# Another order of products at the seams of a two-level Winograd kernel, two attention steps placed earlier, and weight quarters stored in rows of 1 KB

## The chip, the cores and the metric

The kernel runs on one core of a Trainium2 chip. TensorE (PE in the profile) multiplies matrices and writes its results to banks of PSUM; VectorE (DVE), ScalarE (ACT) and GpSimd (POOL) work on them element by element; SyncE (SP) issues the DMAs, one after another in a fixed order. The time of a kernel is the device time of one execution in microseconds (us); times that are compared are medians of several runs. Everything is computed in float32, or in float32r with operands split into parts.

## The reference

A retention layer (linear attention with a decaying state) is followed by a feed-forward layer with ELU:

```python
# q, k, v: (4 batches, 8 heads, 768 positions, 64)
for t in range(S):
    state = gamma * state + k[t] v[t]^T        # per head, 64 x 64
    y[t] = q[t] state / sqrt(64)
x = y as (3072 tokens, 512)                    # the heads side by side
h = x @ w_in                                   # (3072, 2048)
g = where(h > 0, h, exp(min(h, 0)) - 1)
out = g @ w_out                                # (3072, 512)
```

## The kernel before

**Work.** The 3072 tokens are six blocks of 512, each of four chunks of 128. Retention is computed by chunks: scores (k^T q inside stretches of 64 tokens, masked; `scores`, L336), the products k^T v that carry the state (`states`, L385), and the outputs from both (`outputs`, L397). Each is a train of 64x64 matmuls: `scores(tb, pp)` and `states(tb, pp)` treat pair `pp` of the chunks of block `tb`. Their sums and masks are VectorE's (L342, L383), the decay of v is POOL's (`scale_v`, L305).

The two products of the feed-forward layer use Winograd's form of Strassen's scheme: seven products of quarter blocks instead of eight, with sums of blocks before and after. The numbers 1 to 7 in the code name these seven products. Block 0 takes `plain_first` and `second_of_first`. Block 1 takes one level in the first layer (`first(n)`, four entries n = 0 to 3, L772, steps in `strassen`, L734) and two levels in the second (`second_twice`, L953). Blocks 2 and 3, then 4 and 5, are taken together in two **rounds** (`for nb in range(NB)`).

**A round.** In a round's first layer the outer products 2, 1, 3 and 7 are done by a second level, in eight **units** (`ORDER1`: four products, two halves each), each a generator `big_twice` (L1255). Outer products 4 and 6 are done in float32r: `passes` (L1323) multiplies weights and inputs that were split into a high and a low part. Per 128 rows of outputs there is a slice A (first passes of 6, `six`), B (first passes of 4, `four`) and C (the third pass of both). Outer product 5 (`big_rest`, L1309) is plain float32. The **entry** is the place where the units end and the passes begin. After the first passes of a slice VectorE scales the bank and adds another term (`six_sum`, `four_sum`, L917), and only then may the third pass add to that bank. `begin` and `end` are the two halves of an ELU: ScalarE's two operations (L1342, L1343), then VectorE's (L1344). `seeds` are POOL's sums (L1833 to L1837) at the entry. The round's second layer is `second_big` (L1361).

**Inside a unit.** Products 1, 6, 5 and 3 write to bank `pa` (two of these, taken in turn), 2 to `pb`, 7 and 4 to `pd`. ScalarE copies what is needed later (`lift`, L1279), VectorE adds (`plus`, L1283). The unit stops at each `yield`; the loop over `ORDER1` runs the new unit (`cur`) to its next stop, and in between the rest of the one before (`tail`). By that, before the change TensorE's order at a seam is 1 of the new unit, 4 of the old, 2, 6, 7 of the new, 3 of the old, 5 of the new.

**Queues.** The order on every engine is written by hand, by the order of the calls. Weights come in slices of 128x512 or 128x256 from DRAM through a ring of eight buffers (`wq`; eleven in the first layers). `want_first` (L1160) and `want_second` list the slices in the order of use; `done` gives a buffer back when TensorE has read it, and `fetch` (L850) then issues the next slice on the list. SyncE handles its DMAs strictly in order, so a fetch that waits for TensorE holds up what is queued behind it: stores (`send_small`, L679), outputs, and the loads of chunks (`load`, L125). Eight semaphores serve the DMAs in turn, so that each DMA also waits for the landing of the one eight before.

**Parts.** `parts_of_layer` (L919) splits a quarter of a weight block into three planes: ScalarE (L923), VectorE (L917), POOL or VectorE (L925), and two stores. `next_part` (L1701) sends the planes made last and makes the next; it uses two buffers `wp`, so it waits for an earlier store to land. Six of the eight parts are made while `first(1)` to `first(3)` run, in the loop at L1706.

**Raw quarters.** `send_quarters` (L897) stores the blocks of `w_in` for the second round's units, of which product 1 and 2 use halves of one slice (`scratch3[.., 0]`), and product 4 half of another. The first round reads these blocks straight from `w_all`.

Of the kernel before, what the change touches and what calls it, by code (L numbers as in the profile page):

```python
# [28 lines left out]
def kernel(  # L29
# [645 lines left out]
    to_send = []  # L675
# [221 lines left out]
    def send_quarters(j):  # L897

        for at in range(2):
            for k, n, half in ((1, 0, 0), (2, 0, 1), (4, 2, 1)):  # L900
                r, c = {1: (0, 0), 2: (0, 1), 4: (1, 1)}[k]
                to_send.append((
                    scratch3[AMONG[j], at, n][:, 256 * half : 256 * half + 256].rearrange("p (f d) -> p f d", f=2),
                    W_IN[j][:, 2 * r + at, :, c, :],
                ))
# [254 lines left out]
    def want_first(n):  # L1160
# [20 lines left out]
        piece(*before, 3)  # L1181
        for m in range(2 * NQ):
            part("C", m)
            part("B", m)
            if m + 1 < 2 * NQ:
                part("A", m + 1)
            if n and m % 2:
                want((tb, "r", 5, m // 2), scratch4[m // 2])
# [66 lines left out]
    def big_twice(n, j, at):  # L1255
# [3 lines left out]
        def product(k, ps, begin):  # L1259
            which, half = AT[k]  # L1260
            name = (n + 2, "t", j, at, which)
            if n == 0 and k in (1, 2, 4):
                r, c = {1: (0, 0), 2: (0, 1), 4: (1, 1)}[k]
                w = W_IN[j][:, 2 * r + at, :, c, :]
            else:
                w = where[name][:, 256 * half : 256 * half + 256].rearrange("p (f d) -> p f d", f=2)
# [26 lines left out]
        u2 = lift(pa)  # L1293
        pd = bank("d")
# [411 lines left out]
    for n in range(NQ):  # L1706
# [8 lines left out]
        for at in range(2):  # L1715
            next(cur)
        next(tail, None)
# [11 lines left out]
        for at, s in enumerate(cur):  # L1729
            next(sides[n], None)  # L1730
            next(sides[n], None)
            if n and at:
                next_part(n < 3)
# [47 lines left out]
    for s in sec:  # L1781
# [11 lines left out]
        if at in LOADS:  # L1793
            load(3 * CPB + LOADS[at])
            scale_v(3 * CPB + LOADS[at])
        if s == ORDER2[-1]:
            break
    scores(3, 0)
# [8 lines left out]
    for nb in range(NB):  # L1807
# [82 lines left out]
        for at, (j, sub) in enumerate(ORDER1):  # L1890
# [13 lines left out]
            next(cur)  # L1904
            side(at, 1)
            if nb == 0:
                if at == 0:
                    states(3, 0)
                elif at == 1:
                    retention_step(3, 3)  # L1910
            run(tail)
            if at == 7:
                seeds(0, 1, first=True)
            next(cur)
            tail = cur
            if nb == 0:
                if at == 0:
                    scores(3, 1)
# [17 lines left out]
        end("C11", 5)  # L1936
        for n in range(2 * NQ):
# [10 lines left out]
            four(n)  # L1948
# [3 lines left out]
            if n < LAST:  # L1952
                six(n + 1)
            if n:
# [7 lines left out]
            elif n == 1:  # L1962
                end("C11", 6)
            else:
                end("C22", n - 2)
            if n:
                end("C21", n - 1)
# [111 lines left out]
```

## Time and profile before

| | us |
|---|---|
| median of 3 runs | 613.16 |
| the runs | 612.36, 615.98, 613.16 |
| the profiled execution | 612.33 |
| its span | 610.6 |

The stretches of the profiled execution, by the windows of the trace (us from the span's start; shares of the window):

| stretch | what runs there | VectorE busy | DMA share |
|---|---|---|---|
| 133.5 to 190 | `first`, block 1's first layer | 0.88 | 0.87 |
| 190 to 237 | `second_twice` | 0.86 | 0.91 |
| 237 to 259 | first two units, with block 4's retention | 0.75 | 0.64 |
| 259 to 295 | units, round one | 0.90 | 0.94 |
| 295 to 333 | passes, round one | 0.93 | 0.85 |
| 333 to 432 | second layer, round one | 0.82 | 0.59 |
| 432 to 484 | units, round two | 0.73 | 0.52 |
| 484 to 523 | passes, round two | 0.92 | 0.70 |
| 523 to 610 | second layer, round two | 0.77 | 0.54 |

TensorE counts as busy over nearly the whole span, and its granted clock is 1.0 throughout. A float32 matmul of the program is two records in the trace (x8 is a product of four), a float32r one is one record. In the order of time a line shows the start and the length in us, the engine, the line of code, the operation, what it writes and reads, the shapes, how many were merged, and in brackets the idle time before it with what ended it. In the list of waits a line shows who waited for whom, with the total in us, the number of times and the longest. Because matmuls are pipelined, a matmul's own length (379 ns for 128x256) is longer than the distance to the next one (216 ns).

### The profile page before, as it was taken

The page shows a single profiled execution, that of the slowest core. Times are in us where ns is not written, and L with a number is a line of the kernel's source. Part 1 is how long each engine was busy: PE and PEld are TensorE (multiplying, and loading weights), DVE is VectorE, ACT ScalarE, POOL GpSimd, SP SyncE. Part 2 cuts the span into 40 slices and gives each one's busy share as a digit, 9 for nine tenths or more (in the row PEclk, how much of TensorE's full clock was granted, in tenths as well). Part 3 has the DMA queues.
Part 4 walks back from the last instruction along what each step waited for, and adds up shares of the span by engine and source line. Part 5 has one row for each costly group of instructions (what it writes and reads, how often), then busy time and mean ns, then how long its engine had stood idle before and what let it go on. Part 6 is the DMA issues. An engine that isn't in the chain of part 4 may idle for free.

```text
span 610.6 us, 13767 instructions
## 1 busy us (share of the span) xinstructions
PE 602.7 (99%) x5510; PEld 492.5 (81%) x5510; DVE 506.5 (83%) x778; ACT 262.3 (43%) x448; POOL 97.0 (16%) x75
## 2 busy tenths in 40 slices
PE   8999999999999999999999999999999999999997
PEld 6765568888889998888766888888888866788886
DVE  5769889989799886889998787898658999778785
ACT  6899744205553112147689310100236778611110
POOL 2011000000220001000697000110000398000000
PEclk9999999999999999999999999999999999999999
DMA  8698569789977999599986455874554676656553
GB/s 318 272 389 308 172 215 270 234 244 259 353 236 242 296 394 325 182 299 258 307 286 222 125 136 156 271 272 115 191 166 154 172 206 191 166 152 188 152 151 116
DMA packets 87856, 139.85 MB, mean 229 GB/s; under 512 B 7024, under 2 KB 48752, under 8 KB 83056
## 3 DMA queue, kind: packets, MB, share of 16 engines
q1 hardware_dynamic: 87792, 138.96, 71.3%
q8 instruction: 44, 0.72, 0.5%
q14 instruction: 20, 0.16, 0.1%
HBM read 105.12 MB, written 33.82 MB: 228 GB/s over the span
## 4 chain that ended last, share of the span: by engine, by line
PE 92%; DMA 3%; DVE 2%; POOL 1%; issue 0%; ACT 0%; ACTq 0%; DVEq 0%
PE pa L1376 16%; PE pa L1268 8%; PE pd L1376 8%; PE pa L977 4%; PE pb L1376 4%; PE pd L1268 4%; PE pa L557 3%; PE x L647 3%; PE pa L784 3%; PE x L1330 3%; PE pa L647 2%; PE pa L1317 2%; PE pb L1268 2%; PE sc L331 2%; PE pd L977 2%; PE kv L371 2%
## 5 line engine op out<-in xcount | busy, mean ns | idle before, releaser
L1384 ACT COPY ms<-pa 128x256 f32<-128x256 f32 x41 | 15.2, 372 | 107.5 <-PE pa L1376 103.0
L1376 PE MATMUL pa<-gC,wq 128*128 128x256 f32 x240 | 56.8, 382 | 0.0
L1376 PEld LDWEIGHTS pa<-gC,wq 128*128 128x128 f32 x240 | 45.1, 190 | 7.2 <-issue 1.0
L305 POOL TENSOR_TENSOR chunk<-chunk,vf 128x512 f32<-128x512 f32 x15 | 19.1, 1278 | 164.9 <-DMA chunk<-in_qkv_dram 120.2
L1343 ACT ACTIVATE r<-r 128x512 f32<-128x512 f32 x64 | 40.4, 631 | 2.0
L1279 ACT COPY m<-pa 128x512 f32<-128x512 f32 x32 | 18.7, 584 | 38.5 <-PE pa L1268 35.1
L1388 DVE TENSOR_TENSOR res<-pd,ms 128x256 f32<-128x256 f32 x26 | 11.0, 422 | 28.2 <-PE pd L1376 17.4
L1376 PE MATMUL pd<-w_all,wq 128*128 128x256 f32 x120 | 28.3, 379 | 0.0
L1344 DVE SCALAR_TENSOR_TENSOR gC<-r,gC 128x512 f32<-128x512 f32 x24 | 27.6, 1158 | 0.0
L925 POOL TENSOR_TENSOR wp<-wp 128x512 fp32r<-128x512 f32 x6 | 8.4, 1404 | 116.3 <-DMA scratch_dram<-wi 102.8
L1376 PEld LDWEIGHTS pd<-w_all,wq 128*128 128x128 f32 x120 | 22.8, 190 | 3.1
L1833 POOL TENSOR_TENSOR chunk<-chunk,w_all 128x512 f32<-128x512 f32 x4 | 5.1, 1298 | 127.1 <-DVE gC L1348 127.1
L183 ACT ACTIVATE w_all<-wraw 128x1024 uint32<-128x1024 uint32 (+1 forms) x19 | 19.1, 1007 | 14.0 <-PE x L647 9.8
L1358 DVE TENSOR_TENSOR gC<-w_all,gC 128x1024 f32<-128x1024 f32 x20 | 24.2, 1260 | 0.0
L1376 PE MATMUL pa<-ts,wq 128*128 128x256 f32 x96 | 22.9, 381 | 0.0
L1376 PE MATMUL pa<-w_all,wq 128*128 128x256 f32 x96 | 22.9, 381 | 0.0
L185 ACT ACTIVATE w_all<-wraw 128x1024 fp8e4<-128x1024 f32 (+1 forms) x19 | 22.6, 1190 | 0.6
L1376 PE MATMUL pd<-ts,wq 128*128 128x256 f32 x96 | 22.7, 379 | 0.0
L557 PE MATMUL pa<-xb,w_all 128*128 128x512 f32 x48 | 21.5, 597 | 0.0
L1410 ACT COPY res<-pa 128x256 f32<-128x256 f32 x13 | 4.8, 372 | 38.1 <-PE pa L1376 38.1
L213 DVE CUSTOM_DVE_ANT_0 w_all<-wraw,w_all 128x2048 uint16<-128x2048 uint16 (+1 forms) x19 | 20.1, 1057 | 0.8
L514 ACT ACTIVATE r<-r 128x512 f32<-128x512 f32 x32 | 20.2, 630 | 1.0
(361 smaller groups left out, 1606.7 us busy)
## 6 DMA issues: line engine op xcount, KB each, us to landing
wq<-scratch_dram SPq DMA_DIRECT2D x231, 256.0 KB, 3.5
chunk<-in_qkv_dram SPq DMA_DIRECT2D x22, 1024.0 KB, 7.3
wraw<-in_w_dram SPq DMA_DIRECT2D x15, 1024.0 KB, 6.1
scratch_dram<-wp SPq DMA_DIRECT2D x8, 512.0 KB, 4.0
out_dram<-res SPq DMA_DIRECT2D x7, 512.0 KB, 3.4
scratch_dram<-gT SPq DMA_DIRECT2D x12, 256.0 KB, 4.3
wq<-scratch_dram SPq DMA_DIRECT2D x24, 128.0 KB, 3.2
scratch_dram<-w_all SPq DMA_DIRECT2D x24, 128.0 KB, 3.0
```

Source lines behind the costliest of these rows:

```text
L183: nc.scalar.activation(flat, lo, AF.Copy, scale=2.0**-29)
L185: nc.scalar.activation(top, hi.bitcast(FP32), AF.Copy, scale=2.0**-120, saturate=False)
L213: vec.tensor_tensor(out=flat, in0=c, in1=flat, op=ALU.add)
L514: nc.scalar.activation(e, e, AF.Exp, scale=-1.0)
L557: nc.tensor.matmul(hp, lhsT=w[n][:, fi, j // 2, j % 2, :], rhs=xb[:, j, :], start=(j == 0), stop=(j == 3))
L647: nc.tensor.matmul(X[j][:, d, :], lhsT=w[j][:, d * P : d * P + P], rhs=x[j], start=(n == 0 and d == 0), stop=at_end, skip_group_check=True,)
L977: nc.tensor.matmul(ps, lhsT=w[:, f, :], rhs=ts[j][k][:, f, :], start=(begin and f == 0), stop=(f == 3), skip_group_check=True,)
L1268: nc.tensor.matmul(ps[:, f, :], lhsT=w[:, f, :], rhs=big_xs[j][k], start=(begin and f == 0), stop=True, skip_group_check=True,)
L1343: nc.scalar.activation(r, r, AF.Exp, scale=-1.0)
L1344: return lambda: nc.vector.scalar_tensor_tensor(g, r, -1.0, h, ALU.add, ALU.max)
L1358: nc.vector.tensor_tensor(out=quarter(to, r, t), in0=quarter(x, r, t), in1=quarter(y, r, t), op=op)
L1376: nc.tensor.matmul(ps, lhsT=w[:, f, :], rhs=ts[j][k][:, f // 2, f % 2, :], start=(begin and f == 0), stop=(f == 3), skip_group_check=True,)
```

## The change

1. `send_quarters`: the two blocks that share a slice go out in one store whose rows are 1 KB; the slice then holds them interleaved, and `product` reads its half by another index. Per unit pair there are four stores instead of six.
2. `big_twice` gets one more stop, after product 6. With the changed loop the order at a seam becomes 1 of the new unit, 4 of the old, 2, 6 of the new, 3 of the old, 7, 5 of the new (at the last unit, 3 stays behind 7).
3. `first`: the third entry makes one part less, and the fourth makes one more, between its product 1 and the third entry's product 3.
4. Block 4 (`tb` 3): `scores(3, 0)` moves from the end of `second_twice` to the end of its step 4, `states(3, 0)` from the first unit to the end of step 5, and `scores(3, 1)` from behind product 5 of the first unit to ahead of it.
5. The entry: `four(0)` comes ahead of the first third pass and `four(1)` ahead of the first `four` third pass; the list of slices follows (A0, B0, C0, A1, B1, C1, A2, C2, B2 and on instead of A0, C0, B0, A1, C1, B1). Of two ELU ends in one step, the one whose bank is needed first comes first.

```diff
--- before.py
+++ after.py
@@ -897,12 +897,13 @@
     def send_quarters(j):
 
         for at in range(2):
-            for k, n, half in ((1, 0, 0), (2, 0, 1), (4, 2, 1)):
-                r, c = {1: (0, 0), 2: (0, 1), 4: (1, 1)}[k]
-                to_send.append((
-                    scratch3[AMONG[j], at, n][:, 256 * half : 256 * half + 256].rearrange("p (f d) -> p f d", f=2),
-                    W_IN[j][:, 2 * r + at, :, c, :],
-                ))
+            for k, n in ((slice(2), 0), (1, 2)):
+                w = W_IN[j][:, at if n == 0 else 2 + at, :, k]
+                to = scratch3[AMONG[j], at, n]
+                if n:
+                    to_send.append((to[:, 256:512].rearrange("p (f d) -> p f d", f=2), w))
+                else:
+                    to_send.append((to.rearrange("p (f c) -> p f c", f=2), w.rearrange("p f k d -> p f (k d)")))
 
     LAYER = {4: w_b_[:, :, :, 1], 5: w_b_[:, :, :, 0], 6: w_y_}
 
@@ -1179,9 +1180,15 @@
         part = lambda x, m: want((tb, x, m), scratch5[m, "ABC".index(x)])
         part("A", 0)
         piece(*before, 3)
+        part("B", 0)
         for m in range(2 * NQ):
             part("C", m)
-            part("B", m)
+            if m == 0:
+                part("A", 1)
+                part("B", 1)
+                continue
+            if m > 1:
+                part("B", m)
             if m + 1 < 2 * NQ:
                 part("A", m + 1)
             if n and m % 2:
@@ -1263,7 +1270,11 @@
                 r, c = {1: (0, 0), 2: (0, 1), 4: (1, 1)}[k]
                 w = W_IN[j][:, 2 * r + at, :, c, :]
             else:
-                w = where[name][:, 256 * half : 256 * half + 256].rearrange("p (f d) -> p f d", f=2)
+                w = where[name]
+                if which:
+                    w = w[:, 256 * half : 256 * half + 256].rearrange("p (f d) -> p f d", f=2)
+                else:
+                    w = w.rearrange("p (f k d) -> p f k d", f=2, k=2)[:, :, half]
             for f in range(2):
                 nc.tensor.matmul(
                     ps[:, f, :], lhsT=w[:, f, :], rhs=big_xs[j][k], start=(begin and f == 0), stop=True,
@@ -1291,6 +1302,7 @@
         plus(0, 0, pb, m1)
         product(6, pa, False)
         u2 = lift(pa)
+        yield
         pd = bank("d")
         product(7, pd, True)
         m7 = lift(pd)
@@ -1714,6 +1726,8 @@
         cur = first(n)
         for at in range(2):
             next(cur)
+        if n == 3:
+            next_part()
         next(tail, None)
         next(cur)
 
@@ -1729,7 +1743,7 @@
         for at, s in enumerate(cur):
             next(sides[n], None)
             next(sides[n], None)
-            if n and at:
+            if n and at >= (1, 2, 1)[n - 1]:
                 next_part(n < 3)
             if at == 1 and n == 0:
                 some(smalls[2], 2)
@@ -1793,9 +1807,12 @@
         if at in LOADS:
             load(3 * CPB + LOADS[at])
             scale_v(3 * CPB + LOADS[at])
+        if at == (4, "end"):
+            scores(3, 0)
+        elif at == (5, "end"):
+            states(3, 0)
         if s == ORDER2[-1]:
             break
-    scores(3, 0)
     for _ in sec:
         pass
     mid.close()
@@ -1902,20 +1919,22 @@
             if at == 1 and nb == 0:
                 retention_step(3, 2)
             next(cur)
+            if at < 7:
+                run(tail)
+            next(cur)
             side(at, 1)
             if nb == 0:
                 if at == 0:
-                    states(3, 0)
+                    scores(3, 1)
                 elif at == 1:
                     retention_step(3, 3)
-            run(tail)
             if at == 7:
+                run(tail)
                 seeds(0, 1, first=True)
             next(cur)
             tail = cur
             if nb == 0:
                 if at == 0:
-                    scores(3, 1)
                     states(3, 1)
                 elif at == 1:
                     retention_step(3, 4)
@@ -1934,6 +1953,7 @@
         seeds(2, 3, 4, 5, 6, 7)
         six_sum(0)
         end("C11", 5)
+        four(0)
         for n in range(2 * NQ):
 
             passes(nb, n, 6, True, q6[n])
@@ -1945,12 +1965,15 @@
                 begin("C22", n - 2)
             elif n == 0:
                 begin("C11", 6)
-            four(n)
+            if n > 1:
+                four(n)
             if n > 2:
                 end("C12", n - 3)
             four_sum(n)
             if n < LAST:
                 six(n + 1)
+            if n == 0:
+                four(1)
             if n:
                 begin("C21", n - 1)
                 big_rest(nb, n - 1, q6[n - 1])
@@ -1960,11 +1983,11 @@
                 end("C11", 2)
                 end("C11", 3)
             elif n == 1:
+                end("C21", 0)
                 end("C11", 6)
             else:
-                end("C22", n - 2)
-            if n:
-                end("C21", n - 1)
+                for x, m in (("C21", n - 1), ("C22", n - 2))[:: 1 if n % 2 else -1]:
+                    end(x, m)
             if n == 2:
                 end("C11", 7)
             if n > 1:
```

## The prediction, made before the changed kernel was run

> **What bounds the kernel.** I read the page first, then who waited for whom on TensorE, then TensorE's instructions in order of time around each place that the change touches.
>
> ```profile
> span 610.6 us, 13767 instructions
> PE 602.7 (99%) x5510; PEld 492.5 (81%) x5510; DVE 506.5 (83%) x778; ACT 262.3 (43%) x448; POOL 97.0 (16%) x75
> ...
> q8 instruction: 44, 0.72, 0.5%
> ```
>
> TensorE is busy for 602.7 of 610.6 us. The change neither adds nor removes a matmul, so it can only win back what TensorE loses between matmuls. The busy figure hides part of that, because a matmul's modelled end overlaps the next. I therefore go by the distance from start to start: a 128x256 float32 product runs in steps of 216 ns (eight in 1.73 us), a float32r pass in steps of 232. Whatever exceeds this is loss, plus some 100 ns on the step after a wait.
>
> The waits on TensorE between 160 and 310 us, and the same places in the order of time:
>
> ```profile
> PE y L427 <- issue: 0.6, 1, 0.6
> PE sc L331 <- issue: 0.5, 1, 0.5
> ...
> PE pa L784 <- ACT m L726: 0.2, 1, 0.2
> ```
>
> ```profile
> 242.68 1.08 PE L331 MATMUL sc<-chunk 64*64 64x64 f32 x57
> 244.22 0.34 PE L331 MATMUL sc<-chunk 64*64 64x64 f32 x7 [0.46 <-issue]
> ...
> 247.47 0.93 PE L427 MATMUL y<-chunk 64*64 64x64 f32 x48
> 248.96 0.46 PE L427 MATMUL y<-chunk 64*64 64x64 f32 x16 [0.56 <-issue]
> ```
>
> **1. Fourth entry of `first`: a part moved from the third to the fourth.** ScalarE between 166 and 170 us:
>
> ```profile
> 167.13 0.63 ACT L923 ACTIVATE wp<-w_all 128x512 fp32r<-128x512 f32 x1 [2.80 <-DMA scratch_dram<-wp]
> 167.67 0.57 ACT L726 COPY m<-pa 128x512 f32<-128x512 f32 x1
> 169.09 0.63 ACT L923 ACTIVATE wp<-w_all 128x512 fp32r<-128x512 f32 x1 [0.86 <-DMA scratch_dram<-wp]
> 169.63 0.58 ACT L743 COPY pb<-pa 128x512 f32<-128x512 f32 x1
> ```
>
> The part (L923) waits for a store of its buffer to land, and the two copies that TensorE needs stand behind it. TensorE's steps lose 346+104 ns at 168.29 and 145+104 at 170.26: 0.70 us. In the new order both copies of the third entry stand ahead of the part. Product 5 ends at 166.2, so its copy runs from 166.4 to 167.0 and product 3 starts at 167.95 without waiting. L743 follows the part that ends at 167.76, once product 1 has ended (about 168.1 to 168.7); product 2 wants it at 169.7. **-0.70** (bounds -0.70 and 0). The last part still starts at about 173.1 to 173.6, so SyncE's first fetches behind its store don't get later; their first slice landed 2.4 us before its use.
>
> **2. Scores and k^T v of block four.** Both waits above lie in trains of 64x64 matmuls (64 records in about 1 us), and their steps are 674 and 774 ns too long: 1.45 us. They stand 258 instruction words apart in the program (four words to a float32 matmul, one to a wait), and the 44 packets of the instruction queue are 16 KB each, 256 words. Two start at 241.82 and 246.65 and take 0.92 and 0.96; TensorE goes on 1.5 and 1.4 us after each ends. So a block that is run through in less than the lag to its fetch's start (2.7 and 3.2 us here), plus 0.95, plus 1.4 waits. In words the waiting boundaries follow blocks of 4.3 and 3.7 us. In the new order scores(3,0) and states(3,0) stand a step earlier each among products of the third block, in blocks of 7.7, 7.7 and 10 us, and the first waiting boundary is gone; the second follows a block of 4.7 to 4.8 us. At the lags seen it needs 5.0 to 5.5. I take 0.4 us of stall (bounds 0 and 3.3, by the longest lag seen, 4.8).
>
> Rule and row differ here. The Trainium skill (Runtime: NRT & Kernel Launch, "Instruction fetch mechanics") has the same 16 KiB blocks of 256 instructions, but calls the cost of crossing one mostly hidden; no row shows another cause for these two waits, so I follow the row, and the rule's result is rival A.
>
> Costs. One visit more: three trains become four, and a visit costs 94 ns on the step before, 105 on the step after, and 0.08 us (64 records alone take 1.09, within a longer train 1.01): +0.28. The second scores need the last chunk. Its request (SyncE, 233.67) stands behind a fetch that waits for TensorE at 232.21. Both moved trains now run before that, 1.29 us each, so the request goes out at about 236.1, while scores(3,1), now ahead of product 5, reaches that chunk at 242.3. A chunk lands 5.0 us after its request (310.71) to 8.2 (233.67): 241.1 to 244.3. I take 0.1 us, nearest to the rows with little queued ahead (5.0 to 6.5), as the later fetches leave the queues emptier; bounds 0 and 2.0. VectorE gets 1.3 us of sums with each moved train, and TensorE is later by as much: the slack of 0.28 us at pd (read until 225.51, rewritten at 225.78) stays. Sum: -1.45+0.28+0.10+0.40 = **-0.67** (bounds -1.2 and +1.6).
>
> **3. Seams between units.** A unit's product 1 needs the bank of the unit two before it, whose product 3 came just one product earlier (0.86 us), and ScalarE's copy takes 0.1+0.585 plus its signal. The first step of each such product 1 is 295 to 298 ns instead of 216 (276.03, 282.16, 288.28; 447 to 478 five times), and 267.16, 269.89 and 459.18 lose 138, 134 and 124. With product 3 ahead of product 7 it has two products of cover, and pd's sum three instead of two. Product 5 keeps two behind 6. Round one -0.51, round two -0.53: **-1.04** (bounds -1.04 and 0: the copy of 7 now has two products instead of three, enough for 0.7 us). The waits at 260.85, 262.71 and 439.91 are of another order and stay. VectorE's and POOL's orders don't change here.
>
> **4. The rounds' entry.** TensorE and then VectorE:
>
> ```profile
> 296.20 1.02 PE L1268 MATMUL pa<-w_all,wq 128*128 128x256 f32 x4
> 297.23 0.73 PE L1330 MATMUL pa<-xr,wq 128*128 128x512 f32 x2
> ...
> 299.76 0.73 PE L1330 MATMUL pd<-xl,wq 128*128 128x512 f32 x2
> 300.69 0.73 PE L1330 MATMUL pb<-xr,wq 128*128 128x512 f32 x2 [0.20 <-DVE pb L917]
> ```
>
> ```profile
> 296.47 0.70 DVE L917 SCALAR_TENSOR_TENSOR pa<-pa,chunk 128x512 f32<-128x512 f32 x1 [0.31 <-PE pa L1330]
> ...
> 300.54 2.88 DVE L1344 SCALAR_TENSOR_TENSOR gC<-r,gC 128x512 f32<-128x512 f32 x2
> 303.35 0.69 DVE L917 SCALAR_TENSOR_TENSOR x<-x,m 128x512 f32<-128x512 f32 x1
> ```
>
> Each third pass waits for a sum on VectorE that reads the bank just filled; from 294.4 to 300.7 TensorE takes 6.29 us for 5.44 of steps. The new order puts four(0) and four(1), 0.93 us each, into these gaps. C0 then starts at 297.99 (its sum ends at 297.17), the copy at 299.25, its sum at 300.0; six(1) and four(1) fill up to 300.32; C1 ends at 301.25 as before, with four(1) already done: 0.93 won. But VectorE's two sums of 300.54 stay, so the next sum ends at 304.04, and TensorE would want it at 303.9: some 0.2 given back, and a 0.1 restart. C21's sum now stands ahead of C11's, so four(2) starts at 305.35 rather than 305.92. Round two, whose slices land early: -0.60. In round one B1's slice takes the place of one that landed at 300.06, behind a chunk, and is wanted at 299.39, which leaves -0.35. Two small waits before four(4) go, 72 and 55 ns. **-1.08** (bounds -2.0 and 0).
>
> POOL is the reason for the 2.88 us: L1344 takes 0.68 where POOL is between operations and 1.18 to 1.78 while one runs, ending 0.55 us after it. The Trainium skill (SBUF — State Buffer, "Who interferes with whom") says that a VectorE instruction with two SBUF inputs waits out a running GpSimd one that reads SBUF; the trace agrees. By that rule any sum moved ahead in this queue may cost a POOL operation (1.28 us by its rows): rival C.
>
> **5. Rows of 1 KB.** Twenty-four stores become sixteen, and eight issues of about 0.45 us leave SyncE. Bytes and matmuls are the same. A 128 KB store in 512-byte rows lands 0.37 us after the one before, in 1 KB rows (xb) 0.33. Nothing on TensorE waits for these stores: 0 (bounds -0.2 and 0); one fetch also goes out ahead of two wp stores, which costs nothing, as its slice was already seconds early.
>
> **Sum.** -0.70-0.67-1.04-1.08 = -3.5. The profiled execution took 612.33 us (span 610.6 and 1.7 around it): 608.8. The median shown, 613.16, is 0.8 above this execution: **609.7**.
>
> **Rivals.** A: the two issue waits aren't blocks but belong to the trains. Then 1.45 stays and the added visit and the chunk cost 0.38: -2.4, 610.7. For it: "issue" names no cause; against: the 258 words. B: transfers take the place. DMA is busy 0.91 of 190 to 237 us and 0.94 of 259 to 295. The last chunk at 8.2 us costs 2.0, round one's seams and entry win nothing: -0.70+1.23-0.53-0.67 = -0.7, 612.5. Against: TensorE waited for no slice. C, slower: at the rounds' entry VectorE falls behind POOL. C11's third sum now stands behind C21's, where POOL runs. If two more sums a round each wait out a POOL operation with TensorE behind them, 4x1.3 = 5.2 outweighs the 3.5: 614.9; from three such collisions on it decides. Against: from 306 on TensorE never waited for VectorE.
>
> **Chances.** Forecast 0.58 (its own range 608.2 to 611.3), A 0.15, B 0.17, C 0.07, anything else 0.03. 1% is 6.1 us, about what a measurement of this kernel can tell from no change. Winning that needs more than all losses named; losing it needs C twice over or a stalled queue. Range 607.5 to 614.0: the bounds of 2 and 4, and the runs shown, which lie 3.6 us apart.
>
> **What would show it.** Right: steps of 216 ns at 168 to 171 and in product 1 of each unit; no issue wait near 244; the first C1 pass followed at once by six(2). Wrong: scores(3,1) split by a wait for the chunk; an issue wait over 0.8 us in the y train; third passes waiting for VectorE past 306.

## The result, and the profile after

The changed kernel takes **612.05 us** (median of 22 runs, 610.36 to 614.34), the kernel before **613.53** beside it (22 runs, 611.04 to 616.76). The ratio is 0.9968 with a 95% interval of 0.9954 to 0.9983, so 1.0 to 2.8 us were won, where 3.5 had been forecast. The forecast of 609.7 was 2.35 us too low. The result lies outside the forecast's own band (608.2 to 611.3) and inside the stated range (607.5 to 614.0), which is 6.5 us wide.

The two profiled executions don't show this difference: 612.33 us before (1.2 below the median of its kernel) and 612.41 after (0.36 above), both with a span of 610.6. That is of use here, since whatever was won must have been lost again in the same trace, and can be looked up.

Line numbers have moved: L977 is now L978, L1268 is L1279, L1330 is L1342, L1317 is L1329, L1344 is L1356, L917 and L923 are L918 and L924. The page of the changed kernel:

```profile
span 610.6 us, 13757 instructions
PE 601.7 (99%) x5510; PEld 493.7 (81%) x5510; DVE 507.6 (83%) x778; ACT 261.9 (43%) x448; POOL 96.8 (16%) x75
```

TensorE's busy time is 1.0 us less in a span that is the same. So the busy share says nothing here; the distances from start to start do. The table cuts TensorE's work at points that both kernels reach with the same matmuls done (times of the kernel before), and sets beside each stretch what the prediction had for it.

| stretch, by the times before | before | after | change | forecast |
|---|---|---|---|---|
| start to 166.22 (end of the third entry's product 5 in `first`) | 166.22 | 166.28 | +0.06 | 0 |
| to 172.09 (part 1) | 5.88 | 5.18 | -0.70 | -0.70 |
| to 217.74 (rest of block 1's first layer, `second_twice`) | 45.65 | 46.32 | **+0.67** | 0 |
| to 257.02 (end of block four's outputs: part 2) | 39.28 | 40.81 | **+1.53** | -0.67 |
| to 295.08 (units, round one: part 3) | 38.06 | 37.55 | -0.51 | -0.51 |
| to 333.31 (passes, round one: part 4) | 38.23 | 38.00 | -0.23 | -0.42 |
| to 484.38 (second layer; units, round two) | 151.07 | 150.56 | -0.51 | -0.53 |
| to 522.65 (passes, round two) | 38.27 | 38.03 | -0.24 | -0.66 |
| to the end | 84.45 | 84.45 | 0 | 0 |

(The two small waits that part 4 named are put to their rounds.) Three things went as worked out (the first stall, the seams of both rounds), one came out at half (the entry), and two stretches took back 2.2 us.

The waits on TensorE between 160 and 310 us (total, times, longest) are now these:

```profile
PE pd L978 <- DMA wq<-scratch_dram: 0.7, 1, 0.7
PE sc L331 <- issue: 0.5, 1, 0.5
PE pa L978 <- ACT ms L986: 0.4, 1, 0.4
```

The wait for L726 of the list before is gone, and ScalarE's queue shows why; both copies are ready as soon as their bank is:

```profile
166.49 0.58 ACT L726 COPY m<-pa 128x512 f32<-128x512 f32 x1 [2.08 <-PE pa L784]
166.97 0.64 ACT L924 ACTIVATE wp<-w_all 128x512 fp32r<-128x512 f32 x1
168.21 0.57 ACT L743 COPY pb<-pa 128x512 f32<-128x512 f32 x1 [0.61 <-PE pa L784]
```

Some 3 to 15 us later the gain meets VectorE. Before, its queue and the train of k^T v' on TensorE were:

```profile
174.27 0.69 DVE L917 SCALAR_TENSOR_TENSOR wp<-wp,w_all 128x512 fp32r<-128x512 f32 x1 [0.21 <-ACT wp L923]
179.79 2.48 DVE L305 TENSOR_TENSOR chunk<-chunk,vf 128x512 f32<-128x512 f32 x4
181.31 2.08 PE L371 MATMUL kv<-chunk 64*64 64x64 f32 x112
```

After it, ScalarE's first step of the last part, then VectorE's queue in order of time, and TensorE's beside it:

```profile
173.81 0.63 ACT L924 ACTIVATE wp<-w_all 128x512 fp32r<-128x512 f32 x1 [0.89 <-DMA scratch_dram<-wp]
174.48 0.69 DVE L918 SCALAR_TENSOR_TENSOR wp<-wp,w_all 128x512 fp32r<-128x512 f32 x1 [0.58 <-ACT wp L924]
177.59 2.47 DVE L342 TENSOR_TENSOR chunk<-sc,cmask 128x512 f32<-128x512 f32 x4
179.98 2.48 DVE L305 TENSOR_TENSOR chunk<-chunk,vf 128x512 f32<-128x512 f32 x4
182.39 0.67 DVE L731 TENSOR_TENSOR h<-pd,m 128x512 f32<-128x512 f32 x1
...
188.92 0.68 DVE L731 TENSOR_TENSOR h<-pd,m 128x512 f32<-128x512 f32 x1
```

```profile
180.80 2.40 PE L371 MATMUL kv<-chunk 64*64 64x64 f32 x112
...
188.47 1.05 PE L978 MATMUL pa<-ts,wq 128*128 128x128 f32 x8
189.66 1.16 PE L978 MATMUL pd<-ts,wq 128*128 128x128 f32 x8
```

VectorE has no pause from 174.5 to 191 us, and its operations start where they started before (177.39, 179.79, 188.87), although TensorE is 0.63 ahead. It did pause just ahead of that, for 0.58 us: for the last part's first step on ScalarE, which itself waited 0.89 for a store of its buffer to land (173.71). Before, ScalarE's step waited for no store, and VectorE paused 0.21. So the train of k^T v', which needs the scaled v of L305, takes 2.33 us instead of 2.01, and the product at 189.66, which writes the bank that L731 has read until 189.60, starts 0.30 late. At 190 us nothing of part 1 is left.

Around the moved trains, before and after:

```profile
232.93 1.06 PE L977 MATMUL pa<-w_all,wq 128*128 128x128 f32 x8
233.91 1.16 PE L331 MATMUL sc<-chunk 64*64 64x64 f32 x64
235.01 1.16 PE L977 MATMUL pa<-gC,wq 128*128 128x128 f32 x8
```

```profile
236.93 1.06 PE L978 MATMUL pa<-w_all,wq 128*128 128x128 f32 x8
238.34 1.16 PE L978 MATMUL pa<-gC,wq 128*128 128x128 f32 x8 [0.35 <-ACT ms L986]
...
243.85 1.15 PE L331 MATMUL sc<-chunk 64*64 64x64 f32 x61
245.50 0.33 PE L331 MATMUL sc<-chunk 64*64 64x64 f32 x3 [0.49 <-issue]
```

Before, the train of scores(3,0) stood between the two products (233.91), and ScalarE copied the bank while it ran. Now the train is gone from there, the copy is not covered, and the last step ahead of 238.34 is 629 ns instead of 112: 0.52 lost. The last two lines are the wait that was to vanish: the second scores still stop for 0.7 us on the way through a boundary of instruction blocks. The wait in the y train (248.96 before) is gone. Two steps ahead of 218.97 and 220.81 lose 0.29 and 0.88 besides, for weight slices.

A seam of round one. Product 3 of the older unit (274.74) now stands ahead of the newer one's 7 and 5 (275.60, 276.46), and product 1 of the unit after them (277.33) follows without the longer first step; every product takes 0.86:

```profile
274.74 1.03 PE L1279 MATMUL pa<-xt,wq 128*128 128x256 f32 x4
275.60 1.03 PE L1279 MATMUL pd<-tq,wq 128*128 128x256 f32 x4
276.46 1.03 PE L1279 MATMUL pa<-tq,wq 128*128 128x256 f32 x4
277.33 1.03 PE L1279 MATMUL pa<-xb,w_all 128*128 128x256 f32 x4
```

And the entry of round one, TensorE's line and then VectorE's:

```profile
303.19 1.88 PE L1329 MATMUL pa<-xb,w_all 128*128 128x512 f32 x4
305.15 0.73 PE L1342 MATMUL x<-xl,wq 128*128 128x512 f32 x2
```

```profile
300.31 0.70 DVE L918 SCALAR_TENSOR_TENSOR pd<-pd,m 128x512 f32<-128x512 f32 x1 [0.47 <-ACT m L1963]
300.91 0.69 DVE L918 SCALAR_TENSOR_TENSOR pb<-pb,chunk 128x512 f32<-128x512 f32 x1
301.51 2.97 DVE L1356 SCALAR_TENSOR_TENSOR gC<-r,gC 128x512 f32<-128x512 f32 x2
304.41 0.69 DVE L918 SCALAR_TENSOR_TENSOR x<-x,m 128x512 f32<-128x512 f32 x1
```

TensorE has all it needs for the third pass at 304.5 but the sum of x, which ends at 305.10: it stands behind two ELU ends of 1.5 us each, stretched while POOL runs. They start 0.97 later than before (300.54), because the sum of pd, now ahead of them, itself waits for ScalarE's copy.

### The profile page after: what moved, and what is told of

Read it like the earlier page. It is cut to its first block, busy times and chain, and to the rows that moved or that the text cites. A ratio compares the mean times of both kernels' runs of the same rounds, so it can differ in the third digit from the quotient of the medians.

```text
span 610.6 us, 13757 instructions
## 1 busy us (share of the span) xinstructions
PE 601.7 (99%) x5510; PEld 493.7 (81%) x5510; DVE 507.6 (83%) x778; ACT 261.9 (43%) x448; POOL 96.8 (16%) x75
## 4 chain that ended last, share of the span: by engine, by line
PE 90%; DMA 4%; DVE 2%; issue 1%; ACT 1%; SPq 1%; POOL 0%; ACTq 0%; DVEq 0%
PE pa L1388 16%; PE pa L1279 9%; PE pd L1388 8%; PE pd L1279 5%; PE pb L1388 4%; PE pa L557 3%; PE x L647 3%; PE pa L978 3%; PE pa L784 3%; DMA wq<-scratch_dram 3%; PE x L1342 3%; PE pb L1279 2%; PE pa L647 2%; PE y L427 2%; PE y L442 2%; PE pd L1342 2%
## 5 line engine op out<-in xcount | busy, mean ns | idle before, releaser
L305 POOL TENSOR_TENSOR chunk<-chunk,vf 128x512 f32<-128x512 f32 x15 | 18.7, 1256 | 166.0 <-DMA chunk<-in_qkv_dram 102.9
L1355 ACT ACTIVATE r<-r 128x512 f32<-128x512 f32 x64 | 40.4, 631 | 2.0
L1356 DVE SCALAR_TENSOR_TENSOR gC<-r,gC 128x512 f32<-128x512 f32 x24 | 28.1, 1178 | 0.0
```

The source lines that it names most:

```text
L1355: nc.scalar.activation(r, r, AF.Exp, scale=-1.0)
L1356: return lambda: nc.vector.scalar_tensor_tensor(g, r, -1.0, h, ALU.add, ALU.max)
```

## The experiments

Each kernel was measured beside the kernel before on the same chip. Two theories were set against each other at first: **N**, what was won is lost to the engine or copy that is next in line, at places that can be named; **T**, the missing us are transfers that happened to be late in the profiled execution.

**1. The changed kernel again** (no edit).

> The changed kernel unaltered, for a second profile. Theory N (what was won is lost to the next in line): the losses named in the first profile come again at the same places within 0.1 us each: the k^T v' train of 180.8 takes 2.33 us instead of 2.01, the step ahead of 189.66 loses 0.30, the last seam of the third block's second layer 0.5 behind ScalarE's copy, the second scores train 0.7 for issue, and the rounds' entry 0.34+0.3 in each round. Only the wait of 0.9+0.3 us for weight slices at 219 to 221 differs from execution to execution. Theory T (the missing 2 us are late transfers): the second profile lacks most of these, and the span is some 608.5.

Measured: 612.54 (11 runs, 611.82 to 614.14), 0.9980 [0.9965, 0.9995], span 610.6. The train at 181 takes 2.33 again, and this time TensorE also waits 0.84 before it: the store of the last part's buffer landed later, ScalarE waited 1.18 for it, VectorE 0.99 behind ScalarE, and TensorE for L305's v. From 172.1 to 217.7 it is 47.12 us, 0.8 more than in the first profile. The step ahead of the next pd product loses 0.31, the step behind ScalarE's copy 0.52, the passes take 37.99 and 38.00. The second scores lose 0.54 instead of 0.71. Theory N holds for these. But one wait of 0.85 us stands where the first profile had 0.08 (ahead of 234.50, where the read of an instruction block ended 1.48 us earlier), and the slices at 219 cost 0.37 instead of 1.3. So part of the stretch from 217.7 to 257 differs from one execution to the next, and both theories have a share in it.

**2. Part 2 undone.**

```diff
-        if at == (4, "end"):
-            scores(3, 0)
-        elif at == (5, "end"):
-            states(3, 0)
         if s == ORDER2[-1]:
             break
+    scores(3, 0)
...
-                    scores(3, 1)
+                    states(3, 0)
...
                 if at == 0:
+                    scores(3, 1)
                     states(3, 1)
```

> The changed kernel with block four's scores and k^T v' where the kernel before has them. Theory N: the 0.5 us behind ScalarE's copy goes, the visit of 0.28 goes, the chunk is asked for 2.5 us sooner, and two waits for issue (0.67 and 0.77) stand in place of one (0.7): within 0.3 us of the changed kernel, 612.0. The forecast's own reckoning (this part is worth 0.67): 612.7. If the waits for slices at 219 to 221 come from this part, they are gone here; by both theories they are independent of it, as they lie ahead of the first moved train.

Measured: 612.16 (12 runs, 610.22 to 616.56), 0.9986 [0.9964, 1.0007], beside 612.54 for the changed kernel on the same chip. The stretch from 217.7 to 257 takes 38.79, less than in the two executions with the moved trains (40.81 and 40.35) and than before (39.28). The copy is covered again. Of the two old waits for issue one is 0.3 and one hardly there, with the program's words where they were. So these waits are not fixed in size, and part 2 is worth nothing that the times can tell, and not the 0.67. The profiled execution (610.22) is the fastest of these twelve, so its stretch may be shorter than the usual one.

**3. The scalings of v from VectorE to POOL.**

```diff
-            scale_v(2 * CPB, True)
+            scale_v(2 * CPB)
...
-                    scale_v(2 * CPB + m, True)
+                    scale_v(2 * CPB + m)
```

> The changed kernel with the four scalings of v in the third block (L305, 4 x 0.68 us on VectorE, 179.98 to 182.46) on POOL, which is idle from 176.5 to 226. Theory N (VectorE, without a pause from 175.1 to 191, took the 0.7 us that part 1 won): the k^T v' train takes 2.0 us again, the step ahead of 189.66 is 112 ns, and TensorE keeps 0.6 to 0.7 us through 190: 611.3. Rival (something else holds TensorE there, such as a bank or the 0.63 copy on ScalarE): the same 0.6 lost, 612.0; and if POOL, at 1.28 each and ending near 181.7, is late for the train: 0.3 to 0.5 slower.

Measured: 610.72 (6 runs, 610.07 to 612.42), 0.9956 [0.9941, 0.9971]. POOL, VectorE and TensorE of this run:

```profile
176.44 4.49 POOL L305 TENSOR_TENSOR chunk<-chunk,vf 128x512 f32<-128x512 f32 x4
```

```profile
177.55 2.47 DVE L342 TENSOR_TENSOR chunk<-sc,cmask 128x512 f32<-128x512 f32 x4
181.36 0.69 DVE L731 TENSOR_TENSOR h<-pd,m 128x512 f32<-128x512 f32 x1 [1.34 <-ACT m L726]
```

```profile
180.63 2.08 PE L371 MATMUL kv<-chunk 64*64 64x64 f32 x112
```

VectorE now has 1.34 us to spare where it had none, the train takes 2.01 again, and from 172.1 to 217.7 TensorE needs 45.65 us, to the digit what it needed before. The 0.7 is kept. That VectorE's queue held TensorE is shown: in the seven profiles of changed kernels with v on VectorE this stretch takes 46.3 to 47.1 us, in the six with v on POOL (runs 3, 6, 8, 9, 10 and 12) 45.64 or 45.65, but for the waits for issue in runs 8 (0.39) and 12 (1.43). VectorE still waits for the part here (0.59 at 174.44); the 2.5 us taken off its queue make up for it. Whether freeing the part's buffer sooner would have done as well, no run tried. POOL beside them did not slow VectorE's operations either, which here read PSUM and one place in SBUF: L342 takes 2.47 for four with POOL running and without.

**4. One ELU end later at the entry.**

```diff
             if n == 0:
                 end("C11", 2)
-                end("C11", 3)
             elif n == 1:
                 end("C21", 0)
+                end("C11", 3)
                 end("C11", 6)
```

> The changed kernel with C11's fourth end behind C21's first in VectorE's queue at the rounds' entry, so that the sum that the second third pass of four wants (304.41 to 305.10 in the profile) stands behind one ELU end of 1.5 us, not two. Theory N1 (that sum is what holds TensorE): the step ahead of 305.15 falls from 671+333 to 28+637, and the two small waits behind it go: 0.6 us at 309 in each round; 610.8. Theory N2 (VectorE from 297.5 to 308 and ScalarE from 308 to 317 have no room, so their last sums end when they did): the 0.6 comes back as a longer wait at 315.7 and 504.3 (0.3 becomes 0.9): 612.0.

Measured: 613.02 (12 runs, 611.09 to 615.01), 0.9984 [0.9968, 1.0001]. The wait at 305 is gone, and ten us later TensorE waits longer:

```profile
303.29 1.02 PE L1342 MATMUL x<-xl,wq 128*128 128x512 f32 x2
313.06 0.74 PE L1342 MATMUL x<-xl,wq 128*128 128x512 f32 x2 [0.24 <-DVE x L918]
314.58 0.70 PE L1342 MATMUL pd<-xr,wq 128*128 128x512 f32 x2 [0.19 <-PE pa L1342]
```

From the first pass to the second layer it is 38.01 and 38.07 us in the two rounds, as in the changed kernel (38.00 and 38.03). Theory N2 holds: exchanging two ELU ends moves the loss to a later place and does not remove it.

**5. One ELU end sooner, ahead of POOL's seeds.**

```diff
-            (7, 1): [(big_c11, 1, 1)],
+            (7, 1): [(end, "C11", 5), (big_c11, 1, 1)],
...
         six_sum(0)
-        end("C11", 5)
+        end("C11", 2)
...
             if n == 0:
-                end("C11", 2)
                 end("C11", 3)
```

> The changed kernel with C11's first late end moved from the rounds' entry to VectorE's queue ahead of C11's last sum (L1360) in the last unit, before POOL's seeds begin, and the two ends behind it each a place sooner. So one end of 1.5 us stands ahead of the sum that TensorE waits for at 305.1, and everything behind it on VectorE and ScalarE moves up. Theory Q (the ends at the entry, stretched from 0.68 to 1.5 to 1.7 us while POOL runs, are what took part 4's gain): from the first third pass to the second layer 37.1 us instead of 38.0 in each round, no wait at 305 and at 315, 1.8 us in all, span 608.7 from 610.6. Theory R (TensorE's own order or ScalarE's copies hold the entry): 38.0 as before, as in the run with the ends only exchanged; or the end costs its 0.6 us again in the last unit: 0 to 0.3.

Measured: 612.66 (one run), span 610.9. Theory Q fails: 37.93 and 37.88 us instead of 38.00 and 38.03, not 37.1. The waits at 305 and 315 are gone in both rounds, and at 321 TensorE has won 1.1 us on the kernel before; but between 321 and 332 it waits for VectorE again, because there the ends meet POOL's next sums (VectorE's L1356 takes 2.51 at 320.02 and 2.24 at 325.44). Two other orders of the ends have moved the 38 us of passes by 0.0 and 0.1. What the stretch is bound by beyond that, VectorE's and POOL's work together, was not tried by taking work away.

The same run shows the worst of part 2:

```profile
242.31 0.69 PE L331 MATMUL sc<-chunk 64*64 64x64 f32 x32
243.92 0.68 PE L331 MATMUL sc<-chunk 64*64 64x64 f32 x29 [0.92 <-DMA chunk<-in_qkv_dram]
245.87 0.33 PE L331 MATMUL sc<-chunk 64*64 64x64 f32 x3 [1.26 <-issue]
```

The train of the second scores takes 3.82 us instead of 1.09: its second half waits for the last chunk (asked for at 235.25, landed at 243.88), and its last records for the instruction block, whose read started at 243.56.

**6. The three things together**: 3 and 5, and `states(3, 0)` behind the last product.

```diff
         if at == (4, "end"):
             scores(3, 0)
-        elif at == (5, "end"):
-            states(3, 0)
         if s == ORDER2[-1]:
             break
+    states(3, 0)
```

> The changed kernel with the three things that its waits ask for: the scalings of v on POOL (measured above: 0.6 to 0.7 kept), C11's end sooner as in the run beside it (1.8 by theory Q, 0 by R), and states(3,0) kept behind the last product of the third block's second layer, where its train covers ScalarE's copy (0.5). By Q 609.3 against 612.3 for the changed kernel; by R 611.0. The waits for issue may move either by up to 0.8.

Measured: 610.71 (12 runs, 609.49 to 614.23), 0.9954 [0.9930, 0.9978]. The step behind the copy is covered again, and the passes take 37.93 and 37.85. Part 1's gain is kept (45.64). A wait for issue of 0.94 stands at 225.4 this time, in a place where no run had one before. The time lies nearer to R's 611.0 than to Q's 609.3.

**7. The last two chunks cut to an eighth**, to see what holds up the instruction blocks. The kernel leaves out the rest of their input; POOL writes a constant there.

```diff
+        if m in (14, 15):
+            cuts = (0, 256)
+            nc.gpsimd.memset(t[:, 256:2048], 0.5)
         for lo, hi in itertools.pairwise(cuts):
             nc.sync.dma_start(t[:, lo:hi], qkv[m, :, lo:hi])
```

> The changed kernel with only an eighth of the last two chunks loaded (columns 0 to 255 of 2048; POOL fills the rest with a constant), so that 1.8 MB less stand in the transfer queues between 224 and 243 us. It leaves out most of block four's second pair's input. Theory F (an instruction block's fetch waits for what the transfer queues hold): the fetches of the blocks that TensorE enters near 233 and 245, started 6.0 to 6.8 and 7.4 to 9.9 us after the block ahead was entered, start 2 to 4 us after it, and the wait for issue in the second scores train (0.3 to 0.8) is gone. Theory G (a fetch starts by the place reached in the program): it starts as late as before, near 242 to 243, and the wait stays.

Measured: 611.80 (one run). The second scores run through (lines are three higher in this kernel):

```profile
244.08 1.16 PE L334 MATMUL sc<-chunk 64*64 64x64 f32 x64
```

The read of the block entered near 233 to 234 (by the count of words) started 2.1 us after the block ahead was entered; in the four unaltered orders of trains so far (the changed kernel twice, and runs 3 and 4) it was 3.2 to 6.8. The next one, at the second scores, started after 5.9 us instead of 7.4 to 9.9. Both are the lowest of these five profiles, which speaks for F, but the second is above the 2 to 4 that F expected, and run 3 had no wait with full chunks either. One execution does not settle it.

**8 to 10. Beside each other on one chip:** run 3 again; run 3 with part 2 undone as in run 2; and run 3 with the last chunk asked for one step sooner, ahead of one fetch and two stores in SyncE's queue:

```diff
-    LOADS = {(1, "first"): 0, (2, "end"): 1, (4, "end"): 2, (5, "end"): 3}
+    LOADS = {(1, "first"): 0, (2, "end"): 1, (4, "end"): 2, (5, "middle"): 3}
```

> The changed kernel with v scaled on POOL, a second time, as the measure for the two beside it: 610.7 again if the 0.0044 measured was the kernel's and not the chip's. In its profile TensorE keeps part 1's 0.7 us through 217 us; between 217.7 and the end of block four's outputs anything from 39.2 to 41.7 us by the five executions so far with the moved trains.

> The same with block four's scores and k^T v' where the kernel before has them. From the product at 217.74 to the end of block four's outputs at 257.02, the two executions with the old places took 39.28 and 38.79, the five with the new ones 40.81, 40.35, 39.22, 39.43 and 41.72 (mean 40.3). Theory P (the move costs some 1 us where it was to win 0.67: a wait for ScalarE's copy, a visit, and fetches and the last chunk that the transfers hold up): stretch of 38.8 to 39.3, time 1.0 below the run beside it, 609.7. Theory W (only scatter between executions; the move is worth what it was forecast): 0.7 above it, 611.4.

> The changed kernel with v scaled on POOL and the last chunk asked for one step sooner, ahead of a fetch of weights and two stores in SyncE's queue (some 2 us). Theory F (the last chunk's transfer and what queues behind it set when the last instruction blocks come): the chunk lands near 240.5, the block's fetch starts near 240, and neither the chunk (0 to 0.9) nor the issue (0 to 1.3) is waited for in the second scores: 0.4 below the run of the same call without it. Rival: the weight slices behind it land 2.6 us later in a queue that is full, and TensorE waits for them instead near 236 to 241: 0.3 to 1 us above.

| run | median (runs, lowest to highest) | ratio | 172 to 217.7 | 217.7 to 257 |
|---|---|---|---|---|
| 8, v on POOL again | 611.66 (12, 609.94 to 614.25) | 0.9977 [0.9962, 0.9993] | 46.04 | 41.12 |
| 9, part 2 undone | 611.22 (10, 609.33 to 614.32) | 0.9959 [0.9937, 0.9981] | 45.65 | 40.49 |
| 10, chunk sooner | 610.29 (6, 609.53 to 610.99) | 0.9948 [0.9930, 0.9966] | 45.65 | 39.17 |

Run 8 gives 0.9977 where the same kernel gave 0.9956 on another chip, so the three are compared among themselves. The changed kernel itself had 0.9968 and 0.9980: by the times, what v on POOL wins is seen in run 3 and not in run 8, and it rests on the profiles. Run 8's profile has 1.4 us of waits for issue among weights' products (202.81 and 226.63), 0.4 for slices, and 0.2 for the last chunk. Run 9 has 40.49 with the old places, with waits for issue of 0.8 in the old scores and 0.3 in the old y train, and 0.5 for a slice. Neither P (38.8 to 39.3) nor W is met as written: the scatter of a single execution is larger than what part 2 changes. Over all, the six executions with the moved trains and full chunks (both profiles of the changed kernel, runs 3, 4, 5 and 8) have 40.4 on average, the three with the old places (before, 2 and 9) 39.5; by the medians on the two chips that ran both, the old places are 0.4 ahead each time (612.16 to 612.54, 611.22 to 611.66); by the ratios they are 0.4 behind on the first (0.9986 to 0.9980) and 1.1 ahead on the second (0.9959 to 0.9977), all within the intervals. Run 10 is 1.4 below run 8, where F had 0.4, with intervals that just overlap. Its chunk lands at 239.98, and neither the chunk nor an instruction block is waited for in the scores, nor a slice near 236 to 241, as the rival had it; its six runs are also the closest together so far. But the block's read started at 240.97, 8.8 us after the block ahead was entered, and not near 240.

**11 and 12. The chunk sooner alone; and the chunk sooner, v on POOL, and `states(3, 0)` behind the last product.**

> The changed kernel with nothing but the last chunk asked for one step sooner (ahead of a fetch and two stores on SyncE). Theory F (what the moved trains lost from 217 us on is mostly the late chunk and the instruction blocks behind it): the chunk lands near 241 instead of 242.5 to 243.9, the stretch from 217.7 to the end of block four's outputs is 39.2 to 39.6 us instead of 39.2 to 41.7, and the times lie 0.5 to 1 us below the changed kernel's 612.0 to 612.5 and within a narrower span; part 1's 0.7 is still lost to VectorE by 190. Theory W (scatter between executions): 612.3 with the same span of times.

> The chunk asked for sooner, v scaled on POOL (both as measured together: 610.3), and states(3,0) behind the last product of the third block's second layer, where its train stands while ScalarE copies. By the steps of the run with that train there: the 0.52 us at the last seam goes and nothing else moves: 609.8. Rival: the sums of those states on VectorE then come later than the queue has room for, or the block with the train in it is run through sooner and its fetch is waited for (0.3 to 0.8): 610.5.

Run 11: 611.33 (11 runs, 610.80 to 613.35), 0.9950 [0.9932, 0.9968]. That is 0.7 and 1.2 below the two medians of the changed kernel, as F has it, though on another chip, and its runs lie no closer together than run 1's. The chunk lands at 240.44, the scores run through, and the stretch takes 39.03, below the 39.2 to 39.6 that F allowed; from 172 to 217.7 it is 46.34, so part 1's gain is still lost:

```profile
242.92 1.16 PE L331 MATMUL sc<-chunk 64*64 64x64 f32 x64
```

Run 12: **610.00** (6 runs, 609.49 to 610.21), 0.9919 [0.9891, 0.9946]. The kernel before had 614.98 on this chip, more than on the others, so 610.0 against its 613.2 to 614.5 elsewhere, 0.993 to 0.995, is the more careful reading. Its median is the lowest of the series, near the 609.8 expected, and below both kernels. The last seam, with the train where ScalarE copies:

```profile
234.27 1.06 PE L978 MATMUL pa<-w_all,wq 128*128 128x128 f32 x8
235.25 1.16 PE L371 MATMUL kv<-chunk 64*64 64x64 f32 x64
236.35 1.16 PE L978 MATMUL pa<-gC,wq 128*128 128x128 f32 x8
```

From 217.7 to 257 it takes 37.99, the shortest of the series. Its profile still has two stray waits, 1.43 for issue at 203 (so that 172 to 217.7 reads 47.08) and one of 1.2 for a slice at 299.

## Why the prediction was right, and where it was not

The direction, the class (within 1%) and the range were right, and by the prediction's own measure the size was not: -1.5 by the medians, -2.0 by the ratio, -3.5 forecast.

**Part 1** was right at its place (-0.70 forecast, -0.70 measured, and the copies stand as worked out) and wrong in the sum. The step that failed is that the gain was carried to the end with a look at SyncE's fetches alone. What is late next is VectorE: full from 174.5 to 191, which shares by stretch (0.88 for 133.5 to 190) did not show. +0.67 came back. Run 3 shows that this queue held TensorE, by taking 2.5 us off it. Why the queue did not move ahead with TensorE is read from the profile alone: the last part, put at 173.1 to 173.6, started at 173.81 (174.22 in run 1), held by a store of its buffer, and VectorE waited for it. In all thirteen profiles with part 1 that step waits for a store, 0.2 to 1.2 us, and before it did not.

**Part 2** was forecast at -0.67 and is +0.4 by the medians of two chips (-0.4 and +1.1 by the ratios) and +0.9 by the profiles' averages, all within the scatter. Three steps failed. First, "the first waiting boundary is gone": it rested on a lag of at most 4.8 us from entering a block to the start of the next block's read. In the six executions with the moved trains and full chunks the block was entered 4.9 to 6.9 us sooner than before, as planned (232.3 to 234.3, from 239.1), but the read started at 239.7 to 243.6, where it had started at 241.8: the lag was 7.4 to 11.3. The start hung on something else than the program's place, and moving the program did not move it. That words and not trains make the waits (against rival A) was right: they stayed at the same words, and went where the read came early. Counted in TensorE's records of each trace (matmuls, weight loads, waits for semaphores), the two old waits stand 256 apart (the prediction counted 258). Second, the train that was moved away had covered ScalarE's copy; 0.52 was not priced at all. The costs of the visits (+0.28) were. Third, the last chunk was taken at 0.1 with a bound of 2.0: it was in time in both profiles of the changed kernel, and late by 0.92 in run 5 and 0.19 in run 8.

**Part 3** was right in every step: -0.51 and -0.51, forecast -0.51 and -0.53.

**Part 4** had the right mechanism and about half the size: -0.23 and -0.24 for -0.42 and -0.66. The 0.93 was won: in both rounds TensorE starts its first product 5 (L1317, now L1329) 0.98 sooner after the first pass, and the 0.25 allowed in round one for B1's slice was not needed (runs 8 and 12 did wait for a slice near there, 0.7 and 1.2). The mis-sized term is the 0.2 "given back", with 0.1 for a restart. The sum that TensorE would want at 303.9 was put at 304.04; it ended at 305.10, because the ends ahead of it did not start at 300.54 but behind the new sum of pd, at 301.51. The whole price is about 0.4 around 305 and another 0.34 at 315, in each round; at 315.76 the pass waits for bank pd, which VectorE's L1356 reads until 315.66. That is rival C's mechanism (ELU ends behind POOL, with TensorE behind them) at some quarter of its price: two places in each round, at 0.3 to 0.4 each and not 1.3.

**Part 5**: none of the waits on TensorE has one of these stores as its cause, as forecast; it was not tried alone. (The slice that the prediction calls "seconds early" can only have been microseconds early.)

**The rivals.** B (transfers take the place, 612.5) comes nearest in time, and half of it happened: chunk, slices and instruction blocks between 217 and 246. Its other half, that round one's seams win nothing, did not. With what the runs show, the sum is 0 for part 1 (+0.8 in run 1), some +0.4 for part 2, -1.02 for part 3 and -0.47 for part 4: -1.1, inside the measured -1.0 to -2.8.

## What to carry to other kernels

Where a stall goes, follow the gain forward, queue by queue, until an engine has a pause to take it, and look at what that pause waits for: here VectorE's last pause was a wait for a weight part behind a store, after it came 16 us without one, and the gain was gone; four scalings moved to the idle POOL brought it back. A train that is moved leaves a place behind, so look at which copy it covered there. Where single executions scatter by more than a change is worth, try to send the transfer that the work waits for sooner, before moving the work: with the chunk one step sooner the stretch took 39.17 and 39.03 us, against 40.4 on average.

## What was unexpected of the hardware

An instruction block can come very late, and TensorE's restart after it takes nearly the same time. In thirteen waits of 0.4 to 1.5 us (two before, one after, two in run 1, one in 2, 5, 6 and 12 each, two in 8 and 9 each) and one of 0.28 (run 10, 232.79), all between 190 and 262 us, TensorE went on 1.24 to 1.51 us after the 16 KB had been read, which itself took 0.9 to 1.8. Counted in TensorE's records, all fourteen stand a multiple of 256 apart, within one; the one at 234.50 of run 1, which the profile puts down to VectorE's L383, is among them. What varied most was the start of the read, by the count of words from 1.8 to 11.3 us after the block ahead was entered. Five of the thirteen stood among 128x128 products, not in a train.

The Trainium skill (Runtime: NRT & Kernel Launch, "Instruction fetch mechanics") calls the cost of crossing such a boundary mostly hidden. In this kernel it is at most of the 44 boundaries. The reads waited for began between 199 and 247 us, where the DMA share is 0.8 to 1.1 from 200 us on, before and after.

What starts a read stays open. That it waits behind what the transfer queues hold is one possible reason. For it: run 7, with small chunks, and reads that began as a chunk of 1 MB landed (241.82 and 241.87 before; 243.10 and 243.31 after; 243.56 and 243.88 in run 5). Against it: for the block of the second scores, read and landing are within 0.6 us in seven of the fourteen profiles only, and 1.0 to 2.8 us apart, in both directions, in the other seven (239.65 and 242.40 in run 3); and with the chunk sooner the reads of runs 10 and 11 still began 8.8 and 8.0 us after the block ahead was entered, within the 7.4 to 11.3 of the six profiles with a late chunk.
